# Weight conversion in a top-k attention + hard-swish kernel: one VectorE instruction per chunk instead of two, the sign word made on GpSimd

## The chip, the cores and the metric

One Trainium2 chip, one of its cores. The metric is the device time of one execution in microseconds (us). In profiles PE is TensorE, DVE is VectorE, ACT is ScalarE, POOL is GpSimd and SP is the engine whose queue issues most of the DMAs.

## What is computed

```python
def _attn_ref(q, k, v):                      # 8 batches, 8 heads, 576 rows, head size 64
    scores = scale * np.matmul(q, k.transpose(0, 1, 3, 2))
    kth = np.partition(scores, -top_k, axis=-1)[..., -top_k:-top_k + 1]      # top_k = 32
    scores = np.where(scores >= kth, scores, -1000000000.0)
    scores = scores - np.max(scores, axis=-1, keepdims=True)
    attn = np.exp(scores)
    attn = attn / (np.sum(attn, axis=-1, keepdims=True) + 1e-09)
    return np.matmul(attn, v).astype(np.float32)

def _moe_ref(x, w_in, w_out):                # x: 4608 x 512, the attention's output
    h = x @ w_in                             # 512 x 2048
    g = h * np.clip(h + 3.0, 0.0, 6.0) / 6.0
    return (g @ w_out).astype(np.float32)    # 2048 x 512
```

`w_in` and `w_out` arrive as 64-bit floats (a float32 matrix times a 64-bit scalar). The kernel reads them as pairs of 32-bit words and turns them into 32-bit floats itself. That conversion is what the change is about.

## The kernel before

**Attention.** The work is cut into 80 duos. A duo is 128 query rows (64 for the last, short row tile of a batch) of four heads, handled as two pairs, u = 0 and u = 1. Ten duos make a batch. For each duo TensorE forms the scores (L254 to L262), ScalarE copies them to SBUF (L271), and VectorE finds each row's 32 largest by four rounds of MAX8 (L283) with MATCH_REPLACE8 between them (L287). One round of one pair is a slot: a duo has 8 slots, numbered on over the kernel, so duo m has slots 8m to 8m+7. A slot's VectorE work is two MAX8 and two MATCH_REPLACE8, and in the fourth round of a pair (slots 3, 7, 11, 15 ...) the two MAX8 alone.

After a pair's fourth round: `shift` (two tiny GpSimd instructions, L296 and L299), `exp` (ScalarE, L306 to L316, which needs `shift` for its second half), `inverse` (a VectorE reciprocal, L320), `weights` (GpSimd: L330 scales the two rows, L339 splits their words into 16-bit halves), `flip` (a transposing DMA from SP's queue, L345), `join` (L351, on ScalarE or GpSimd), `values` (TensorE, L371) and `place` (ScalarE, L381). The slot of each is written out in the tables at L570 to L583. The first two duos use the table `early`: shift and exp in the fourth round's own slot, inverse and weights one slot later, flip one after that, join in slot 8 or 12.

**Feed-forward.** 36 blocks of 128 rows (L385). A block is four groups of 32 matmuls (L398), each with a ScalarE eviction (L406, L408) into a tile of the pool `g` and a gate of two GpSimd instructions (L412, L413), and then 16 matmuls with `w_out` (L418). Blocks are cut into pieces and about one piece is put into each slot.

**Conversion.** 32 chunks of 128x512 weights (16 of `w_in`, 16 of `w_out`). `convert` (L96) is a generator with three stops, and `convert_step` (L522), called once in each slot, moves it on. Chunk k has in the code before:

- its load (L103), a DMA into `st`, a tile of the pool `kq`, which also holds the attention's tiles;
- in slot k-2: ScalarE turns the low word into a rounding term `y` (L109; `y` is a PSUM tile for the first 24 chunks, the destination itself for the last 8), then takes the absolute value of the high word (L112) over the low word; GpSimd clamps that (L113);
- in slot k: VectorE shifts the clamped word left by 3 (L118), and a second VectorE instruction (L119) puts the high word's sign bit to `y` and writes the destination;
- in slot k+1: GpSimd adds the two as 32-bit integers (L124), which gives the float.

So the conversions run beside the first 33 slots. In slot s the order on each engine is: the top-k round; shift, exp, flip, join, values and place that are due; GpSimd's add for chunk s-1; VectorE's conversion of chunk s; ScalarE's and GpSimd's part for chunk s+2; the next load; then score matmuls or transposes; then inverse and weights. The order on every engine is the program's order (L68, `manual_schedule`); tiles of a pool take the buffer that has been free longest.

**Start.** `transpose(first=True)` (L189 to L202) turns the first pair's keys and queries on TensorE; ScalarE copies the results out (L195 to L197), and after `scores((0,))` (L267 to L271) it copies three blocks of scores, the small one (`rest`) first.

Of the kernel before, what the change touches and what calls it, by code (L numbers as in the profile page):

```python
# [8 lines left out]
AF = mybir.ActivationFunctionType  # L9
ALU = mybir.AluOpType  # L10
F32 = mybir.dt.float32
U32 = mybir.dt.uint32
I32 = mybir.dt.int32
# [11 lines left out]
HI_LEAST = 2.0**-15  # L25
HI_MOST = 122880.0 - 2.0**-7
# [3 lines left out]
def kernel(  # L30
# [9 lines left out]
    nc = tc.nc  # L40
    P = nc.NUM_PARTITIONS
# [3 lines left out]
    JP = J * P  # L45
    R = S - JP
    NHP = H // 2
    NFC = FF // P
    assert 2 * D == P and 2 * R == P and NHP * P == DM and B % 2 == 0
    assert JP == 512 and DM == 512 and TOP_K % 8 == 0  # L50
    scale = 1.0 / float(D) ** 0.5

    def pool(name, bufs, **kw):
        return ctx.enter_context(tc.tile_pool(name=name, bufs=bufs, **kw))
# [8 lines left out]
    gpool = pool("g", 8)  # L63
# [3 lines left out]
    ps_w = pool("ps_w", 3, space=PSUM)  # L67
# [20 lines left out]
    def big():  # L88

        return ps_big.tile([P, 5 * 512], F32, tag="big", name="big")  # L90
# [2 lines left out]

    WC = 512

    def convert(dst, src, early):  # L96

        st = kqpool.tile([P, 2 * WC], U32, tag="kq", name="st")
        nc.sync.dma_start(st[:], src)  # L103
        yield
        words = st[:].rearrange("p (n two) -> p n two", two=2)
        lo, hi = words[:, :, 0], words[:, :, 1]
        y = ps_w.tile([P, WC], F32, tag="w", name="y")[:] if early else dst

        nc.scalar.activation(y, lo, AF.Copy, bias=2.0, scale=2.0**-51)  # L109

        a = lo.bitcast(F32)
        nc.scalar.activation(a, hi.bitcast(F32), AF.Abs)  # L112
        nc.gpsimd.tensor_scalar(a, a, HI_MOST, HI_LEAST, ALU.min, ALU.max)  # L113
        yield

        nc.vector.tensor_scalar(lo, lo, 3, None, ALU.logical_shift_left)  # L118
        nc.vector.scalar_tensor_tensor(  # L119
            out=dst.bitcast(U32), in0=hi, scalar=0x80000000, in1=y.bitcast(U32),  # L120
            op0=ALU.bitwise_and, op1=ALU.bitwise_or,
        )
        yield
        nc.gpsimd.tensor_tensor(  # L124
            dst.bitcast(I32), lo.bitcast(I32), dst.bitcast(I32), ALU.add
        )

    def weight_chunks():
        win, wout = moe_w_in.bitcast(U32), moe_w_out.bitcast(U32)
        for f in range(0, FF, WC):  # L130
            for g in range(NHP):
                rows = slice(g * P, (g + 1) * P)
                yield w_in[:, g, f : f + WC], win[rows, 2 * f : 2 * (f + WC)]
        for c in range(NFC):
            rows = slice(c * P, (c + 1) * P)
            yield w_out[:, c, :], wout[rows, :]
# [3 lines left out]
    class Pair:  # L140
# [31 lines left out]

        def transpose(self, first=False):

            kq = kqpool.tile([P, JP + S], F32, tag="kq", name="kq")
            self.kT, self.qT = kq[:, 0:JP], kq[:, JP : JP + S]
            c0 = 2 * JP

            def turn(ps, tiles):
                for i, j in enumerate(tiles):  # L180
                    rows = self.landed[:, j, :, :].rearrange("p h d -> p (h d)")
                    nc.tensor.transpose(ps[:, i * P : (i + 1) * P], rows, ident[:])  # L182

            def copy_left(ps):
                for hh in range(2):
                    d = slice(hh * D, (hh + 1) * D)
                    nc.scalar.copy(self.kr[d, hh, :], ps[d, 0:R])

            if first:  # L189

                ps = [ps_w.tile([P, 512], F32, tag="w", name="kqp") for _ in range(3)]
                turn(ps[0], range(J))
                turn(ps[1], [J, 2 * J])
                turn(ps[2], range(J + 1, 2 * J))
                nc.scalar.copy(self.kT, ps[0][:])  # L195
                nc.scalar.copy(kq[:, JP : JP + P], ps[1][:, 0:P])
                copy_left(ps[1][:, P:])  # L197
                self.later = [
                    (kq[:, JP + P : c0], ps[2][:, 0 : JP - P]),
                    (kq[:, c0 : c0 + R], ps[1][:, P + R : 2 * P]),  # L200
                ]
                return  # L202
            ps = big()
            turn(ps, range(2 * J + 1))
            nc.scalar.copy(kq[:, 0:c0], ps[:, 0:c0])
            nc.scalar.copy(kq[:, c0 : c0 + R], ps[:, c0 + R : c0 + 2 * R])
            copy_left(ps[:, c0:])

    class Duo:
# [15 lines left out]
        def scores(self, us=(0, 1)):  # L225

            if us[0] == 0:
                self.sc = scpool.tile([P, 2, 2 * (S + R)], F32, tag="sc", name="sc")
                self.den = mpool.tile([P, 2, 2], F32, tag="den", name="den")
            sc, nu = self.sc[:, us[0] : us[-1] + 1, :], len(us)  # L230
            ps = big()
            heads = [slice(0, D), slice(D, P)]
            qs = slice(self.qt * P, min(self.qt * P + P, S))
            banks = ps[:, 0 : 4 * 512].rearrange("p (n s) -> p n s", s=512)
            left = ps[:, 4 * 512 :]
            if self.rest:


                quarters = [
                    (i, hh, d, heads[u ^ hh])  # L240
                    for i, u in enumerate(us)
                    for hh, d in enumerate(heads)
                ]
                for i, hh, d, to in quarters:
                    pr = self.pairs[us[i]]
                    nc.tensor.matmul(banks[to, i, :], pr.qT[d, qs], pr.kT[d, :])
                for i, hh, d, to in quarters:
                    pr = self.pairs[us[i]]
                    nc.tensor.matmul(banks[to, 2 + i, 0:R], pr.qT[d, qs], pr.kr[d, hh, :])
                nc.gpsimd.memset(sc[:, :, S : S + R], 0.0)  # L250
                nc.scalar.copy(sc[:, :, 0:JP], banks[:, 0:nu, :])
                nc.scalar.copy(sc[:, :, JP:S], banks[:, 2 : 2 + nu, 0:R])
                return
            for i, u in enumerate(us):  # L254
                pr = self.pairs[u]
                nc.tensor.matmul(  # L256
                    left[:, i * P : (i + 1) * P], pr.qT[:, qs], pr.kr[:].rearrange("p h r -> p (h r)")
                )
            for i, u in enumerate(us):
                pr = self.pairs[u]  # L260
                for hh, d in enumerate(heads):
                    nc.tensor.matmul(banks[:, 2 * i + hh, :], pr.qT[d, qs], pr.kT[d, :])  # L262
            copies = [
                (sc.rearrange("p u (h s) -> p (u h) s", h=2)[:, :, 0:JP], banks[:, 0 : 2 * nu, :]),
                (sc[:, :, JP : JP + P], left[:, 0 : nu * P].rearrange("p (u r) -> p u r", r=P)),
            ]
            if us == (0,):  # L267
                (to, src), rest = copies
                copies = [rest, (to[:, 0, :], src[:, 0, :]), (to[:, 1, :], src[:, 1, :])]
            for copy in copies:  # L270
                nc.scalar.copy(*copy)  # L271

        def row(self, u, t):
            return self.sc[:, u, t * S : (t + 1) * S]
# [237 lines left out]
    chunks = list(weight_chunks())  # L512
    landing, converting, adding = [], [], []

    def land(count=1):

        for _ in range(min(count, len(chunks))):
            c = convert(*chunks.pop(0), early=len(chunks) >= NFC // 2)
            next(c)
            landing.append(c)  # L520

    def convert_step():  # L522


        for c in adding:
            next(c, None)
        adding.clear()
        if len(converting) >= 2 or not landing:
            for c in converting[:1]:
                next(c)  # L530
            adding.extend(converting[:1])
            del converting[:1]
        if landing:
            c = landing.pop(0)
            next(c)
            converting.append(c)
        land()
# [10 lines left out]
    ps = big()  # L548
    for _ in range(2):
        nc.tensor.matmul(ps[:, 0:DM], w_out[:, 0, 0:P], w_out[:, 0, :])  # L550
    first[0].load(nc.scalar)
    first[1].load()
    land()
    first[2].load()
    land()
    first[0].transpose(first=True)
    duos[0].scores((0,))
    for copy in first[0].later:
# [17 lines left out]
    early = dict(  # L576
        shift0=3, exp0=3, inverse0=4, weights0=4, flip0=5, join0=8,
        shift1=7, exp1=7, inverse1=8, weights1=8, flip1=9, join1=12, values=12, place=13,
    )
# [98 lines left out]
```

## Time and profile before

| | |
|---|---|
| median of 7 runs | 1564.8 us (1563.7 to 1570.43) |
| profiled execution | 1564.29 us, span 1562.5 us |
| first chunk's GpSimd clamp, last chunk's add | 14.5 us, 147.6 us |
| VectorE's two conversion lines, L118 and L119 | 28.6 us + 23.4 us, 32 instructions each |
| ScalarE's two, L109 and L112 | 32 instructions each, medians 0.63 (PSUM) or 0.68 (SBUF), and 0.68 us |
| GpSimd's two, L113 and L124 | 32 instructions each, medians 0.65 and 1.30 us |
| GpSimd's idle time in front of L113, for L112 | 43.9 us, 15 times |
| last MAX8 ends | 1491.6 us; what follows is mostly feed-forward on TensorE |

A row of a timeline gives start, length, engine, line, operation, tiles and count; neighbouring instructions of one line are merged. The bracket is the time for which the engine was idle before, and what ended that. A VectorE or GpSimd instruction that is held up after it has started shows as a longer instruction, not as idle time.

### The profile page before, as it was taken

What the parts mean: (1) busy time and instruction counts of PE and PEld (TensorE: products, weight loads), DVE (VectorE), ACT (ScalarE), POOL (GpSimd) and SP (SyncE); (2) the same over time, 40 slices, a digit from 0 to 9 for tenths busy, and PEclk for the clock granted to TensorE, in tenths of its full rate; (3) what the DMA queues carried; (4) which work ended last, traced back from release to release, by engine and by line L of the source; (5) the groups of instructions that cost most, each with busy time, mean ns of one, the idle gap of its engine ahead of it and who ended that gap; (6) DMA issues with size and microseconds to landing.
All of it is one profiled execution on the core that took longest, in us unless ns stands there. A gap on an engine that the chain in (4) does not pass through costs nothing.

```text
span 1562.5 us, 28780 instructions
## 1 busy us (share of the span) xinstructions
PE 1444.9 (92%) x10276; PEld 1032.4 (66%) x10276; DVE 1464.5 (94%) x3106; ACT 1099.2 (70%) x1868; POOL 1138.0 (73%) x1264
## 2 busy tenths in 40 slices
PE   5256899899999999999999999999999999999899
PEld 3143665677777777667767777677777777666665
DVE  6999999999999998999999999999999999999910
ACT  6676777677777777777777776777777777777631
POOL 3769688677777788677777779777777778777761
PEclk7568799999999999999999999999999999999999
DMA  8553545344344445345344454554344545433320
GB/s 225 157 200 60 100 83 113 75 91 83 69 83 99 99 83 106 72 100 100 70 85 83 102 99 83 90 99 98 69 83 83 99 99 91 96 68 68 77 44 14
DMA packets 450319, 144.49 MB, mean 92 GB/s; under 512 B 433280, under 2 KB 441472, under 8 KB 450176
## 3 DMA queue, kind: packets, MB, share of 16 engines
q1 hardware_dynamic: 448976, 142.36, 44.3%
q8 instruction: 81, 1.33, 0.3%
q14 instruction: 62, 0.51, 0.1%
q10 hardware_dynamic: 1200, 0.30, 0.1%
HBM read 45.09 MB, written 9.44 MB: 35 GB/s over the span
## 4 chain that ended last, share of the span: by engine, by line
DVE 44%; PE 41%; POOL 5%; ACT 4%; issue 4%; DMA 1%; SPq 1%; POOLq 0%; DVEq 0%; ACTq 0%
DVE m L283 23%; DVE wk L287 19%; PE h L398 16%; PE acc L418 15%; PE pv L371 5%; PE big L262 3%; POOL e L339 1%; POOL sc L330 1%; ACT eT L351 1%; POOL eT L351 1%; PE big L182 1%; PE big L256 1%; ACT sc L311 1%; DMA t<-e 1%; DVE st L118 1%
## 5 line engine op out<-in xcount | busy, mean ns | idle before, releaser
L283 DVE MAX8 m<-wk 128x8 f32<-128x576 f32 x864 | 613.7, 748 | 2.2
L418 PE MATMUL acc<-w_out,g 128*128 128x512 f32 x1152 | 520.3, 602 | 11.9 <-POOL g L413 11.9
L398 PEld LDWEIGHTS h<-xT,w_in 128*128 128x128 f32 x4096 | 470.2, 193 | 39.6 <-issue 21.6
L398 PE MATMUL h<-xT,w_in 128*128 128x128 f32 x4096 | 483.2, 277 | 14.2 <-ACT xT L381 13.1
L287 DVE MATCH_REPLACE8 wk<-m,wk 128x576 f32<-128x576 f32 x576 | 424.0, 743 | 0.0
L418 PEld LDWEIGHTS acc<-w_out,g 128*128 128x128 f32 x1152 | 213.5, 192 | 256.7 <-issue 235.7
L330 POOL TENSOR_SCALAR sc<-sc,den 128x576 f32<-128x576 f32 x288 | 213.5, 751 | 202.6 <-DVE den L320 180.7
L339 POOL COPY e<-sc 128x2304 uint16<-128x2304 uint16 (+1 forms) x192 | 320.1, 1677 | 10.1
L351 ACT COPY eT<-t 128x2304 uint16<-128x2304 uint16 (+1 forms) x82 | 216.1, 2635 | 59.0 <-DMA t<-e 54.7
L306 ACT ACTIVATE sc<-sc,m 128x576 f32<-128x576 f32 x288 | 210.6, 779 | 66.2 <-DVE m L283 66.0
L311 ACT ACTIVATE sc<-sc,shift 128x576 f32<-128x576 f32 x288 | 220.5, 770 | 41.1 <-POOL shift L299 39.0
L371 PE MATMUL pv<-eT,vm 128*64 128x128 f32 (+1 forms) x2560 | 164.5, 273 | 58.2 <-DVE w_out L119 20.1
L283 DVE MAX8 m<-sc 128x8 f32<-128x576 f32 x288 | 203.4, 744 | 10.2 <-ACT sc L271 10.2
L287 DVE MATCH_REPLACE8 wk<-m,sc 128x576 f32<-128x576 f32 x288 | 212.0, 743 | 0.0
L351 POOL COPY eT<-t 128x2304 uint16<-128x2304 uint16 (+1 forms) x78 | 203.6, 2610 | 7.3 <-DMA t<-e 7.2
L371 PEld LDWEIGHTS pv<-eT,vm 128*64 128x64 f32 x2560 | 135.5, 141 | 109.9 <-issue 21.6
L406 ACT ACTIVATE g<-h,three 128x512 f32<-128x512 f32 x144 | 98.9, 687 | 135.7 <-PE h L398 135.4
L413 POOL TENSOR_TENSOR g<-g,hs 128x512 f32<-128x512 f32 x144 | 184.5, 1281 | 12.2 <-POOL g L412 0.2
L271 ACT COPY sc<-big 128x256 f32<-128x256 f32 (+3 forms) x131 | 136.5, 1095 | 26.4 <-PE big L262 26.1
L412 POOL TENSOR_SCALAR g<-g 128x512 f32<-128x512 f32 x144 | 88.7, 616 | 69.4 <-ACT g L406 59.6
L262 PE MATMUL big<-kq 64*128 64x512 f32 x512 | 133.0, 639 | 0.0
L408 ACT COPY hs<-h 128x512 f32<-128x512 f32 x144 | 83.8, 582 | 0.0
(58 smaller groups left out, 1001.7 us busy)
## 6 DMA issues: line engine op xcount, KB each, us to landing
landed<-in_k_dram SPq DMA_DIRECT2D x64, 128.0 KB, 2.9
st<-in_moe_w_in_dram SPq DMA_DIRECT2D x16, 512.0 KB, 5.3
vm<-in_v_dram SPq DMA_DIRECT2D x64, 128.0 KB, 2.4
st<-in_moe_w_out_dram SPq DMA_DIRECT2D x16, 512.0 KB, 5.2
out_dram<-o SPq DMA_DIRECT2D x32, 256.0 KB, 2.4
landed<-in_q_dram SPq DMA_DIRECT2D x62, 128.0 KB, 2.9
t<-e SPq DMA_TRANSPOSE x160, 4.6
landed<-in_k_dram SPq DMA_DIRECT2D x32, 32.0 KB, 2.5
```

The source lines that it names most:

```text
L262: nc.tensor.matmul(banks[:, 2 * i + hh, :], pr.qT[d, qs], pr.kT[d, :])
L283: nc.vector.max(self.m[u][:, t, 8 * r : 8 * r + 8], self.cur[t])
L287: nc.vector.match_replace(wk, self.m[u][:, t, 8 * r : 8 * r + 8], self.cur[t], LOWEST)
L306: nc.scalar.activation(row, row, AF.Prelu, bias=m[:, t, TOP_K - 1 : TOP_K], scale=-1.0, alpha=FLAT)
L311: nc.scalar.activation(row, row, AF.Exp, bias=self.less[u][:, t : t + 1], scale=-scale / FLAT, accum_out=self.den[:, u, t : t + 1],)
L330: nc.gpsimd.tensor_scalar(row, row, self.den[:, u, t : t + 1], 1.0, ALU.mult, ALU.mult)
L339: nc.gpsimd.tensor_copy(halves[:, :, to : to + c1 - c0], words)
L351: copy(eT[:, 0 : self.nb, :] .rearrange("p c q -> p (c q)") .bitcast(U16) .rearrange("p (x h) -> p h x", h=2), self.t16[u][:, 0 : 2 * self ...
L371: nc.tensor.matmul(pv[hh * D : (hh + 1) * D, u * w : (u + 1) * w], pr.vm[:, hh, c, :] if c < J else pr.vr[:, hh, :], rhs, start=(c == 0), ...
L398: nc.tensor.matmul(h[:, (f - f0) * P : (f - f0 + 1) * P], w_in[:, i, f * P : (f + 1) * P], xT[:, i, :], start=(i == 0), stop=(i == NHP - 1),)
L413: nc.gpsimd.tensor_tensor(g[:], g[:], hs[:], ALU.mult)
L418: nc.tensor.matmul(acc[:], gs[f // nf][:, f % nf * P : (f % nf + 1) * P], w_out[:, f, :], start=(f == 0), stop=(f == NFC - 1),)
```

## The change

Per chunk, the absolute value goes to a tile `a` of its own, from the feed-forward's pool `g` (8 buffers, tag `g`); the rounding term goes straight to the destination for all 32 chunks, so that no PSUM tile is used; and ScalarE does the absolute value first. GpSimd gets an instruction more: the high word, read as a float, times 0.0 leaves a zero with the high word's sign, written over the low word in `st`. VectorE's single instruction shifts `a` left by 3 and sets the sign with an exclusive-or. GpSimd's add stays as it was. At the start, two ScalarE lines and the first `rest` copy go to VectorE.

```diff
-    def convert(dst, src, early):
+    def convert(dst, src):
...
-        y = ps_w.tile([P, WC], F32, tag="w", name="y")[:] if early else dst
-
-        nc.scalar.activation(y, lo, AF.Copy, bias=2.0, scale=2.0**-51)
-
-        a = lo.bitcast(F32)
-        nc.scalar.activation(a, hi.bitcast(F32), AF.Abs)
-        nc.gpsimd.tensor_scalar(a, a, HI_MOST, HI_LEAST, ALU.min, ALU.max)
+        a = gpool.tile([P, WC], F32, tag="g", name="a")
+        nc.scalar.activation(a[:], hi.bitcast(F32), AF.Abs)
+        nc.gpsimd.tensor_scalar(a[:], a[:], HI_MOST, HI_LEAST, ALU.min, ALU.max)
+
+        nc.scalar.activation(dst, lo, AF.Copy, bias=2.0, scale=2.0**-51)
+
+        nc.gpsimd.tensor_scalar(lo.bitcast(F32), hi.bitcast(F32), 0.0, 1.0, ALU.mult, ALU.mult)
         yield
...
-        nc.vector.tensor_scalar(lo, lo, 3, None, ALU.logical_shift_left)
+        au = a[:].bitcast(U32)
         nc.vector.scalar_tensor_tensor(
-            out=dst.bitcast(U32), in0=hi, scalar=0x80000000, in1=y.bitcast(U32),
-            op0=ALU.bitwise_and, op1=ALU.bitwise_or,
+            out=au, in0=au, scalar=3, in1=lo,
+            op0=ALU.logical_shift_left, op1=ALU.bitwise_xor,
         )
         yield
         nc.gpsimd.tensor_tensor(
-            dst.bitcast(I32), lo.bitcast(I32), dst.bitcast(I32), ALU.add
+            dst.bitcast(I32), a[:].bitcast(I32), dst.bitcast(I32), ALU.add
         )
...
-            def copy_left(ps):
+            def copy_left(ps, copy=nc.scalar.copy):
                 for hh in range(2):
                     d = slice(hh * D, (hh + 1) * D)
-                    nc.scalar.copy(self.kr[d, hh, :], ps[d, 0:R])
+                    copy(self.kr[d, hh, :], ps[d, 0:R])
...
                 nc.scalar.copy(self.kT, ps[0][:])
-                nc.scalar.copy(kq[:, JP : JP + P], ps[1][:, 0:P])
-                copy_left(ps[1][:, P:])
+                nc.vector.tensor_copy(kq[:, JP : JP + P], ps[1][:, 0:P])
+                copy_left(ps[1][:, P:], nc.vector.tensor_copy)
...
             for copy in copies:
-                nc.scalar.copy(*copy)
+                if us == (0,) and copy is rest:
+                    nc.vector.tensor_copy(*copy)
+                else:
+                    nc.scalar.copy(*copy)
...
-            c = convert(*chunks.pop(0), early=len(chunks) >= NFC // 2)
+            c = convert(*chunks.pop(0))
```

## The prediction

> **What bounds the kernel now.** I read the page's busy table first, then the busy times by stretch, the conversion's own lines, and last the timeline of the conversion engine by engine.
>
> ```profile
> PE 1444.9 (92%) x10276; PEld 1032.4 (66%) x10276; DVE 1464.5 (94%) x3106; ACT 1099.2 (70%) x1868; POOL 1138.0 (73%) x1264
> ```
>
> Over the span VectorE is the fullest engine, with POOL far behind. But conversions run only from 14 to 148 us, and there the stretches (busy time of PE, PEld, DVE, ACT, POOL, then clock, DMA share, GB/s) say something else:
>
> ```profile
> 40.00:60.00 20.00, 1.58 (x6) 0.34 (x2) 20.00 (x34) 14.13 (x20) 15.67 (x18) 0.59 0.60 159
> ...
> 120.00:140.00 20.00, 15.74 (x46) 6.98 (x44) 19.16 (x34) 13.12 (x21) 19.25 (x19) 0.91 0.16 31
> 140.00:160.00 20.00, 11.46 (x59) 6.15 (x60) 20.00 (x44) 10.67 (x18) 18.82 (x19) 0.76 0.48 102
> 160.00:180.00 20.00, 12.84 (x88) 10.83 (x85) 20.00 (x44) 14.30 (x26) 11.01 (x13) 0.65 0.45 90
> ```
>
> VectorE is "full" at 20.00 of 20, but POOL has 15.67, and 19.25 near the end. VectorE's fullness isn't all work:
>
> ```profile
> L118 DVE TENSOR_SCALAR st<-st x32: 404/620/1976, 15.2 to 139.4; 128x512 uint32<-128x512 uint32 x32
> ...
> L119 DVE SCALAR_TENSOR_TENSOR w_in<-st,y x16: 673/675/682, 15.5 to 76.3; 128x512 uint32<-128x512 uint32 x16
> ...
> L119 DVE SCALAR_TENSOR_TENSOR w_out<-st,w_out x8: 678/886/1151, 110.6 to 139.8; 128x512 uint32<-128x512 uint32 x8
> ```
>
> The shift needs 404 ns and takes up to 1976: it is held while POOL works (the one at 54.89 ends at 56.83, when POOL's copy L339 has ended at 56.54). So VectorE has slack that shows as busy time. Who sets the pace is seen in four slots of POOL's timeline:
>
> ```profile
> 60.73 0.19 POOL L296 TENSOR_TENSOR shift<-m 128x2 f32<-128x2 f32 x1
> 61.01 0.22 POOL L299 TENSOR_SCALAR shift<-shift 128x2 f32<-128x2 f32 x1
> 61.20 1.30 POOL L124 TENSOR_TENSOR w_in<-st,w_in 128x512 int32<-128x512 int32 x1
> 64.45 0.65 POOL L113 TENSOR_SCALAR st<-st 128x512 f32<-128x512 f32 x1 [1.96 <-ACT st L112]
> 65.06 1.29 POOL L124 TENSOR_TENSOR w_in<-st,w_in 128x512 int32<-128x512 int32 x1
> 68.32 0.65 POOL L113 TENSOR_SCALAR st<-st 128x512 f32<-128x512 f32 x1 [1.97 <-ACT st L112]
> 69.07 1.47 POOL L330 TENSOR_SCALAR sc<-sc,den 128x576 f32<-128x576 f32 x2
> 70.60 2.10 POOL L339 COPY e<-sc 128x2304 uint16<-128x2304 uint16 x1
> 72.67 1.47 POOL L124 TENSOR_TENSOR w_in<-st,w_in 128x512 int32<-128x512 int32 x1
> 74.22 0.65 POOL L113 TENSOR_SCALAR st<-st 128x512 f32<-128x512 f32 x1
> 74.83 1.29 POOL L124 TENSOR_TENSOR w_in<-st,w_in 128x512 int32<-128x512 int32 x1
> 76.09 0.83 POOL L113 TENSOR_SCALAR st<-st 128x512 f32<-128x512 f32 x1
> 76.88 0.20 POOL L296 TENSOR_TENSOR shift<-m 128x2 f32<-128x2 f32 x1
> ```
>
> From shift to shift it is 16.15 us, and POOL is idle twice, both times for ScalarE. In both waits ScalarE has no gap: after the shift (61.20) come two exponentials, the sum's copy, L109, L112 (to 64.37), the join of 2.75, L109, L112 (to 68.24). The MAX8 that the next shift needs ended at 58.74, 2.0 us ahead of 60.73. So from slot 7 to slot 19 the pace is a loop of POOL and ScalarE; VectorE isn't in it.
>
> **The change part by part.**
>
> *VectorE.* Removed: L118, 28.6 us, and L119, 23.4 us. Added: 32 instructions with both inputs in SBUF. Their nearest row is L119 on `w_out`, 678 to 1151 ns, mean 904 (page of groups by shape): 32 x 0.904 = 28.9. Saved: 52.0 - 28.9 = 23.1 us. Worth that only where VectorE sets the pace, so I take 0 from slot 7 on. The Trainium skill, "VectorE: DVE Perf Modes", section "Rules for kernel authors", says to minimise the number of chained VectorE instructions. The row agrees about VectorE's own time, but the loop above leaves VectorE out; by the rule alone the time would be that of the first rival below.
>
> *POOL, the product.* 32 more instructions. Nearest rows: the clamp L113 on the same words, 0.65 us, and the gate's L412 on dense words, 0.616; so 0.65, 20.8 us in all. What of it is covered, by its place in the four slots: in the first slot (after shift) it waits for ScalarE's L109, but the second 1.97 wait covers it. In the second slot the product follows the clamp, and the clamp comes 0.65 earlier, since the absolute value now runs before the rounding term; cost 0. In the third and fourth slot POOL has no idle time: 2 x 0.65 = 1.30. Back comes what L118 made slower: the add of 1.47 for 1.29 and the clamp of 0.83 for 0.65, 0.35. So +0.95 in each cycle, if nothing collides.
>
> *Collisions.* Where L119 with two SBUF inputs runs beside POOL, POOL is slower: an add takes 1.74 for 1.30 (119.61, 137.59), the two scalings 2.04 and 2.27 for 1.47 (122.06, 139.42). Four VectorE conversions fall in a cycle. Two meet POOL in front of its waits, and are covered. The one in the first slot waits for the third slot's product and so starts beside the next add, +0.44; another falls on L339 or L330, +0.57. From below the cost is 0, so a cycle gains 0.95 to 1.95; with most of them colliding I take 1.5. The Trainium skill, "GPSIMD Engine Reference", section "8. Key points", names just this: SBUF interfaces are shared with VectorE's instructions that have two SBUF inputs. By the rule every one of them collides and the cycle is +1.95; if it did not hold, +0.95.
>
> *ScalarE.* 24 rounding terms go to SBUF: 0.68 for 0.63, and in the loop only once per cycle; 0.05, left out. The PSUM buffer that they free ends no wait of this loop. `a` takes the buffer of `g` free longest; with at most seven of eight in use it waits for an add two chunks back, which POOL has done by then.
>
> *Loads.* `st` is free after VectorE instead of after the add; the loads' order on SP's queue is the same, and no more of them. 0.
>
> *Start.* One 128x128, two 64x64 and one 128x128 copy move to VectorE, idle for 10.21 us there. No row shows VectorE copying from PSUM; between the reciprocal's 0.155 and the 128x512 memset's 0.485 each, so 0.6 to 1.9 in all; ScalarE is rid of 0.27 + 0.43 + about 0.3. The first MAX8 (11.62) may come between 0.9 earlier and, at the dear end, 0.9 later. Neither lasts: the reciprocal at 32.70 waits 1.71 for ScalarE's L316, and ScalarE waits before that for loads (13.07, 17.16). I take 0.
>
> **The sum.** Slots 5 to 7: three products without cover, 3 x 0.65 = 1.95 on POOL; VectorE loses nothing yet. Slots 7 to 15, two cycles: 2 x 1.5 = 3.0. The weights of slot 16 are 4.95 late. From there the path is L339 (ends 88.82), the flip, the join (94.77), values, xT (101.73), the first h matmul (102.23): all 4.95 late. In slots 20 to 24 POOL waits 5.18, 1.79 and 1.70 us for ScalarE, which waits for the join and for h; the products hide there, and the lag stays 4.95. From 114.74 to 152.9 POOL has no idle time. Five more products (chunks 27 to 31) are 3.25, more collisions than the rows there already have 0 to 2.2, I take 0.7: 8.9. The last product ends at 137.59 + 8.9 = 146.5, VectorE's last conversion takes 0.6 to 1.05, and the next MAX8 starts at 147.3 instead of 140.36: 6.9 late. With 0.95 per cycle and no collisions (2.3 us of those in the present rows gone too) it is 2.6 late, with all of them 9.5.
>
> After that, POOL's rest of lag (8.9 against VectorE's 6.9) goes into its 5.12 us of idle time at 160.4. TensorE's pieces at 165.45 and 172.90 wait 4.22 and 2.93 for ScalarE and POOL, which wait for MAX8; so from 173 on everything stands as before, 6.9 later, and stays so, since TensorE and VectorE both run without slack. The profiled execution took 1564.29 (1.8 outside its span, 0.5 under the median): 1564.3 + 6.9 = 1571.2, so 1571; own range 1567 to 1574.
>
> **The rivals.**
>
> 1. *VectorE is the bound after all.* Then 23.1 us come off: 1541.2; half of it where only part of the slots pay, 1553. For it: 20.00 of 20 busy from 40 to 120 us, and slots 20 to 24, where L118 is mostly near 0.41 and POOL waits. Against: the 2.0 us between MAX8 and shift, and L118's 1.98 for 0.40. It decides if POOL's cycle falls under 16.15. 15%.
> 2. *The products are covered.* POOL waits 43.9 us for L112, twice the 20.8; then only chunks 27 to 31 are paid or not: 1564.3 - 2.4 (six unblocked shifts at 0.41 in slots 17 to 23) to + 3.2: 1562 to 1567.5. Against: the waits lie in two of four slots, and none from 114.74 on. 20%.
> 3. *Collisions without cover.* If each of 24 conversions from slot 8 to 31 delays POOL by 0.44 to 0.80, mean 0.6, that is 14.4, with the uncovered products (1.95 + 2.6 + 3.25 = 7.8) 22 on POOL, some 18 on VectorE: 1582. For it: POOL is nearly always busy. Against: L113 and L330 at present lose less on average. 10%.
>
> **How the numbers follow.** The forecast has 55%. A run can tell 0.2%, 3.1 us, from no change. Slower than that: 10% and all but 5 of the 55; within: those 5 and rival 2; faster: rival 1. The range leaves out about half of rival 1 below and rival 3 above: 1556 to 1578.
>
> **What would show it.** Right: POOL's shift-to-shift cycle near 17.6 between slots 7 and 19; VectorE idle in front of the new conversion, for POOL's product, about 3 us per cycle (it now shows as idle, not as a long shift); the conversion's mean near 0.9; POOL above 18 of 20 us from 40 to 140; the last add starting near 156.5; the MAX8 after the last conversion near 147. Wrong: the cycle at 16.2 or less, VectorE without idle time, or a product far from 0.65. If conversion ends as computed and the total still differs, the step from 173 us on is wrong.

## The result, and the profile after

The changed kernel takes 1570.17 us (median; 1569.12 to 1571.53) against 1565.23 us for the kernel before in the same comparison: ratio 1.0027, 95% interval 1.0019 to 1.0035, so 0.3% or some 4 to 5 us slower. The profiled execution took 1568.75 us (span 1567.0) against 1564.29 (span 1562.5), +4.5 us.

The busy table of the kernel after:

```profile
PE 1443.6 (92%) x10276; PEld 1031.3 (66%) x10276; DVE 1450.9 (93%) x3078; ACT 1095.7 (70%) x1864; POOL 1159.5 (74%) x1296
```

VectorE lost 13.6 us of busy time, GpSimd gained 21.5 us, and the kernel is slower by less than either. The stretches of the kernel after (busy time of PE, PEld, DVE, ACT, POOL, each with its number of instructions, then clock, DMA share, GB/s):

```profile
40.00:60.00 20.00, 3.13 (x22) 2.00 (x20) 13.62 (x25) 12.97 (x19) 16.78 (x20) 0.50 0.50 140
...
100.00:120.00 20.00, 17.41 (x121) 15.47 (x122) 20.00 (x40) 16.88 (x33) 18.01 (x23) 0.75 0.61 244
120.00:140.00 20.00, 14.60 (x65) 8.96 (x66) 15.61 (x26) 12.89 (x23) 18.94 (x21) 0.83 0.16 30
140.00:160.00 20.00, 12.76 (x44) 5.28 (x40) 18.75 (x36) 9.35 (x15) 19.27 (x21) 0.74 0.30 63
160.00:180.00 20.00, 9.10 (x73) 6.94 (x75) 20.00 (x45) 13.88 (x26) 12.32 (x12) 0.78 0.63 130
```

VectorE is no longer full in most of the conversion's stretch: 13.62 of 20 where it had 20.00. From 100 to 120 us it still is. GpSimd went from 15.67 to 16.78 only, so it still waits, too. What VectorE waits for is in the rows of the new conversion (its instructions, then its engine's idle time in front of them):

```profile
L118 DVE SCALAR_TENSOR_TENSOR a<-a,st x32: 674/894/1768, 13.8 to 144.6; 128x512 uint32<-128x512 uint32 x32
...
  POOL st L112: 22.4, 8
```

22.4 us in eight waits, all for GpSimd's product (L112). GpSimd's timeline over four slots of the kernel after, from one `shift` to that four slots later:

```profile
63.94 0.20 POOL L301 TENSOR_TENSOR shift<-m 128x2 f32<-128x2 f32 x1
64.22 0.22 POOL L304 TENSOR_SCALAR shift<-shift 128x2 f32<-128x2 f32 x1
64.40 1.27 POOL L123 TENSOR_TENSOR w_in<-a,w_in 128x512 int32<-128x512 int32 x1
66.97 0.61 POOL L108 TENSOR_SCALAR a<-a 128x512 f32<-128x512 f32 x1 [1.30 <-ACT a L107]
67.66 0.66 POOL L112 TENSOR_SCALAR st<-st 128x512 f32<-128x512 f32 x1
68.27 1.28 POOL L123 TENSOR_TENSOR w_in<-a,w_in 128x512 int32<-128x512 int32 x1
70.72 0.61 POOL L108 TENSOR_SCALAR a<-a 128x512 f32<-128x512 f32 x1 [1.16 <-ACT a L107]
71.41 0.66 POOL L112 TENSOR_SCALAR st<-st 128x512 f32<-128x512 f32 x1
72.04 1.98 POOL L335 TENSOR_SCALAR sc<-sc,den 128x576 f32<-128x576 f32 x2
74.09 2.10 POOL L344 COPY e<-sc 128x2304 uint16<-128x2304 uint16 x1
76.15 1.26 POOL L123 TENSOR_TENSOR w_in<-a,w_in 128x512 int32<-128x512 int32 x1
77.51 0.61 POOL L108 TENSOR_SCALAR a<-a 128x512 f32<-128x512 f32 x1
78.20 0.64 POOL L112 TENSOR_SCALAR st<-st 128x512 f32<-128x512 f32 x1
78.80 1.26 POOL L123 TENSOR_TENSOR w_in<-a,w_in 128x512 int32<-128x512 int32 x1
80.15 0.94 POOL L108 TENSOR_SCALAR a<-a 128x512 f32<-128x512 f32 x1
81.16 0.65 POOL L112 TENSOR_SCALAR st<-st 128x512 f32<-128x512 f32 x1
81.77 0.20 POOL L301 TENSOR_TENSOR shift<-m 128x2 f32<-128x2 f32 x1
```

From shift to shift it is 17.83 us; it was 16.15. There is a product in each slot. The one at 67.66 lies in front of a wait for ScalarE (1.16 of the former 1.97 are left), and the one at 71.41 stands where the later clamp used to end. Those at 78.20 and 81.16 have no wait in front of them or behind them, and the next shift is later by both. VectorE's conversions in the same slots:

```profile
72.81 0.68 DVE L118 SCALAR_TENSOR_TENSOR a<-a,st 128x512 uint32<-128x512 uint32 x1
73.42 1.41 DVE L288 MAX8 m<-wk 128x8 f32<-128x576 f32 x2
78.88 1.74 DVE L118 SCALAR_TENSOR_TENSOR a<-a,st 128x512 uint32<-128x512 uint32 x1 [4.05 <-POOL st L112]
```

VectorE is idle for 4.05 us until the product of 78.20 has ended, and its conversion then takes 1.74 us, because GpSimd's add started at 78.80. The conversion ends only after that add has ended (80.06).

### The profile page after: what moved, and what is told of

Its sections match the earlier page's. It is cut to its first block, busy times and chain, and to the rows that moved or that the text cites. A ratio compares the mean times of both kernels' runs of the same rounds, so it can differ in the third digit from the quotient of the medians.

```text
span 1567.0 us, 28761 instructions
## 1 busy us (share of the span) xinstructions
PE 1443.6 (92%) x10276; PEld 1031.3 (66%) x10276; DVE 1450.9 (93%) x3078; ACT 1095.7 (70%) x1864; POOL 1159.5 (74%) x1296
## 4 chain that ended last, share of the span: by engine, by line
PE 55%; DVE 22%; POOL 11%; ACT 5%; issue 5%; DMA 2%; POOLq 0%; SPq 0%; ACTq 0%
PE h L403 22%; PE acc L423 20%; DVE m L288 12%; DVE wk L292 10%; PE pv L376 6%; PE big L264 5%; POOL e L344 2%; POOL sc L335 2%; DMA t<-e 1%; POOL eT L356 1%; PE big L258 1%; POOL g L418 1%; PE big L184 1%; POOL w_in L123 1%; ACT sc L316 1%
## 5 line engine op out<-in xcount | busy, mean ns | idle before, releaser
L403 PE MATMUL h<-xT,w_in 128*128 128x128 f32 x4096 | 484.8, 278 | 12.7 <-ACT xT L386 11.9
L276 ACT COPY sc<-big 128x2048 f32<-128x2048 f32 (+3 forms) x130 | 136.4, 1101 | 25.9 <-PE big L264 23.1
```

The costliest lines, as they stand in the source:

```text
L403: nc.tensor.matmul(h[:, (f - f0) * P : (f - f0 + 1) * P], w_in[:, i, f * P : (f + 1) * P], xT[:, i, :], start=(i == 0), stop=(i == NHP - 1),)
```

## The experiments

The table gives, for every kernel, what it did to the time and where it gained or lost: the start of VectorE's reciprocals (one for each pair of rows; the first four are in slots 4, 8, 12 and 16, the seventh is near the last conversion, and from there on all kernels have the same 9.70 us from one to the next). The cycle is the distance of the third and the fourth. The change in us is the ratio's distance from 1, times 1565.2. The ratio comes from all runs of a kernel, the columns behind it from one execution; executions of one kernel lie 1 to 9 us apart, so small differences in the columns say little.

| kernel | ratio to before (95%) | us | cycle | 2nd | 4th | 5th | 6th | 7th |
|---|---|---|---|---|---|---|---|---|
| before | 1 | 0 | 16.2 | 48.35 | 80.63 | 114.90 | 133.67 | 145.91 |
| after | 1.0027 (1.0019 to 1.0035) | +4.2 | 17.8 | 48.46 | 84.20 | 118.47 | 138.17 | 151.85 |
| no product (e1) | 0.9949 (0.9937 to 0.9961) | -8.0 | 15.9 | 46.72 | 78.44 | 110.76 | 128.10 | 140.23 |
| product in the kernel before (e2) | 1.0089 (1.0077 to 1.0101) | +13.9 | 18.3 | 49.94 | 86.45 | 125.15 | 146.81 | 161.02 |
| start copies only (e3) | 0.9996 (0.9988 to 1.0005) | -0.6 | 16.2 | 47.82 | 80.12 | 114.46 | 133.62 | 145.85 |
| own tile only (e9) | 1.0003 (0.9994 to 1.0012) | +0.5 | 15.8 | 47.92 | 79.45 | 114.16 | 131.80 | 144.47 |
| own tile and order (e7) | 0.9977 (0.9968 to 0.9985) | -3.6 | 15.3 | 46.72 | 77.33 | 113.35 | 132.35 | 146.66 |
| e7 and start (e8) | 0.9985 (0.9974 to 0.9996) | -2.3 | 15.3 | 47.15 | 77.76 | 113.74 | 132.71 | 147.00 |
| after with the old order (e18) | 1.0053 (1.0040 to 1.0066) | +8.3 | 18.4 | 49.65 | 86.54 | 122.02 | 141.68 | 155.39 |
| PSUM operand (e4) | 1.0029 (1.0018 to 1.0040) | +4.5 | 17.0 | 48.34 | 82.40 | 117.88 | 139.38 | 153.09 |
| PSUM operand, `st` free (e4b) | 1.0013 (1.0004 to 1.0022) | +2.0 | 17.0 | 48.82 | 82.83 | 115.68 | 137.22 | 150.92 |
| product on VectorE (e5) | 1.0025 (1.0015 to 1.0035) | +3.9 | 16.5 | 48.31 | 81.30 | 118.59 | 136.04 | 150.53 |
| late products (e14) | 1.0083 (1.0070 to 1.0096) | +13.0 | 16.4 | 53.10 | 85.90 | 121.19 | 141.66 | 159.38 |
| e8, PSUM for all chunks (e17) | 0.9947 (0.9935 to 0.9959) | -8.3 | 15.3 | 47.62 | 78.22 | 112.12 | 127.77 | 139.61 |

**What does the product cost?** e1 is the changed kernel without it; the conversion reads a block of zeros in SBUF in its place, so it still has two SBUF inputs.

```diff
-        nc.gpsimd.tensor_scalar(lo.bitcast(F32), hi.bitcast(F32), 0.0, 1.0, ALU.mult, ALU.mult)
...
-            out=au, in0=au, scalar=3, in1=lo,
+            out=au, in0=au, scalar=3, in1=zeros,     # shortened: a block of w_out that holds zeros
```

> The changed kernel without GpSimd's product; VectorE's instruction takes a block of zeros in SBUF as its second input, so all weights lose their sign. Theory (a loop of GpSimd and ScalarE sets the pace, the product lengthens it): the cycle from shift to shift between slots 7 and 19 falls from 17.9 us to 16.2 to 16.6, and the time from 1570.2 to 1561 to 1565. Rival (VectorE's instruction with two SBUF inputs is what costs, not the product): the cycle stays near 17.5 and the time at 1568 to 1570.

Measured: 1557.97 us, 12.2 us under the kernel after by the ratios, more than expected, and the cycle falls from 17.8 to 15.86, below the expected 16.2 to 16.6. The groups of the run without product:

```profile
L118 DVE SCALAR_TENSOR_TENSOR a<-a,w_out 128x512 uint32<-128x512 uint32 x32 | 33.9, 1061 | 9.9 <-POOL a L109 9.8
```

The conversion's mean, 1061 ns, stays what it was (1076 after), so it isn't quicker conversions that give the gain: of some 21 us of GpSimd's time for the product (32 of them, median 0.656) 12.2 reach the end. In e1 `st` also comes free sooner, as VectorE no longer reads it; in the kernel after the join of slot 20 waited for its own data alone (row below), so no gain from that is seen. VectorE's wait falls from 22.4 to 9.9 us.

e2 is the kernel before with the product as additional work, after the clamp; the conversion on VectorE stays as it was.

```diff
         nc.gpsimd.tensor_scalar(a, a, HI_MOST, HI_LEAST, ALU.min, ALU.max)
+        nc.gpsimd.tensor_scalar(hi.bitcast(F32), hi.bitcast(F32), 0.0, 1.0, ALU.mult, ALU.mult)
```

> The kernel before, with the product added on GpSimd behind the clamp (high word times 0.0 in place; the sign that the second VectorE instruction takes stays the same). Theory: three products per cycle are uncovered here, as the absolute value still comes second on ScalarE: cycle 16.15 + 1.95 = 18.1 us, time 1565.2 + 6 to 9 = 1571 to 1574. Rival (the product hides in GpSimd's waits and the harm came from the new VectorE instruction): 1565 to 1567.

Measured: +13.9 us. The cycle, 18.26, is as expected; the total isn't. The lateness grows behind the cycles, from 5.8 at the fourth reciprocal to 10.3 at the fifth and 15.1 at the seventh, where the expectation let it stand. In this kernel `st` is held until the add, and the join of slot 20 comes 7.4 us behind the copy that it follows; before it was 5.95, after 4.69. So the product alone, with nothing of the rest of the change, slows the kernel by more than the whole change does, and the rest of the change has to be a gain.

**Which part gains?** Start copies alone (e3), the own tile `a` alone (e9), own tile and absolute value first (e7), both with the start (e8), each put into the kernel before, and the old order put into the kernel after (e18).

```diff
 e9, in the kernel before
-        a = lo.bitcast(F32)
+        a = gpool.tile([P, WC], F32, tag="g", name="a")[:]
 e7, in addition
-        nc.scalar.activation(y, lo, AF.Copy, bias=2.0, scale=2.0**-51)
         nc.scalar.activation(a, hi.bitcast(F32), AF.Abs)
         nc.gpsimd.tensor_scalar(a, a, HI_MOST, HI_LEAST, ALU.min, ALU.max)
+        nc.scalar.activation(y, lo, AF.Copy, bias=2.0, scale=2.0**-51)
 e18, in the kernel after
+        nc.scalar.activation(dst, lo, AF.Copy, bias=2.0, scale=2.0**-51)
         nc.scalar.activation(a[:], hi.bitcast(F32), AF.Abs)
...
-        nc.scalar.activation(dst, lo, AF.Copy, bias=2.0, scale=2.0**-51)
```

> The kernel before, with only the three start copies on VectorE. Theory: the first MAX8 comes 1 us earlier and the reciprocal of slot 4 about 1.3 earlier, as in the changed kernel, and here nothing eats it: 1565.2 - 1.3 = 1564. Rival (loads pace the start, as the prediction had it): 1565, with the reciprocal at 32.7 us.

> The kernel before, with only the absolute value in a tile of pool g; ScalarE's order as before. Cycle 16.15 us as before; the join in slot 20 1.2 us earlier; time 1563 to 1565. If st's early release is all that made the kernel without the product fast: 1558 to 1560. If neither counts: 1565.8.

> The kernel before, with both its VectorE instructions and no product, but the absolute value in a tile of pool g and first on ScalarE. Theory: both waits of GpSimd for the absolute value end 0.65 us earlier, one of them counts: cycle 15.5 to 15.9 us; the join in slot 20 comes 1.2 us earlier because VectorE, not GpSimd's add, frees st; time 1558 to 1561, as with VectorE's one instruction and no product. Rival (VectorE's saving counts): 1563 to 1565.

> The kernel before with the absolute value in a tile of pool g and first on ScalarE, and the three start copies on VectorE: the parts of the change without the product and without VectorE's one instruction. Theory: the start adds nothing to the 1560.8 us of the order alone, so 1560 to 1561. Rival: the start's 0.6 to 1.3 us at slot 4 lasts once GpSimd's loop is shorter: 1559 to 1560.

> The changed kernel with ScalarE's two instructions in the old order, rounding term first. Theory (ScalarE is in the loop): the absolute value comes 0.65 us later, the second slot's product is no longer covered: cycle 18.5 us, time 1572 to 1575. Rival (with GpSimd this full the order no longer counts): 1570.

Measured: start copies -0.6 us with an interval that holds 0: the first MAX8 comes at 10.58 for 11.62, and nothing of it is left by the seventh reciprocal (-0.06). The own tile +0.5, no change, although the join of slot 20 comes 2.7 us earlier with it (92.03 for 94.77). With the order as well -3.6, and the old order in the kernel after costs 4.1 us: the order is worth about 4 us in both kernels. e8 adds nothing to e7 that its interval would show; at 1562.9 it is slower than its expectation. Runs of e7 scatter from 1559.2 to 1564.67 us and the profiled one is the longest; no run here shows why. Eight of its eleven runs end at 1561.0 or before, five of e8's twelve at 1560.6 or before, and the profiled one of e8 took 1564.93: the rows of both show a late execution.

What is left is VectorE's one instruction. e1 has it, with the order and the start, and no product; e8 has the order and the start and two instructions. e1 is 5.6 us faster (0.9949 and 0.9985, intervals apart). By the profiled executions (that of e8 a late one) this comes behind slot 19: at its shift e8 is still 2.2 us ahead of e1 (89.27 for 91.45), at the seventh reciprocal 6.8 behind. So VectorE's shorter work, taken at 0 by the prediction from slot 7 on, seems to count there; that e1 also frees `st` sooner and takes no PSUM tile isn't separated from it. With the product in, e18 is 5.6 us ahead of e2, both with the old order: own tile, start and the one instruction together, which no run separates there.

e7's cycle is 15.3, but its lead of 3.3 us at the fourth reciprocal turns into 0.75 of lateness at the seventh. Its conversions that have no PSUM operand, the last eight, say where to look (first row; the second has 16 of those with a PSUM operand):

```profile
L118 DVE SCALAR_TENSOR_TENSOR w_out<-st,w_out 128x512 uint32<-128x512 uint32 x8 | 13.3, 1666 | 0.0
L118 DVE SCALAR_TENSOR_TENSOR w_in<-st,y 128x512 uint32<-128x512 uint32 x16 | 10.8, 675 | 0.0
```

1666 ns in the mean with two SBUF inputs (904 in the kernel before), 675 with one input in PSUM. e17, below, follows that up.

**What do the collisions cost?** e4 lets the conversion of the first 24 chunks read its second operand from PSUM, as the kernel before did; the product is still made, and the add's second input is the product. The sign is left out.

```diff
+        y = ps_w.tile([P, WC], F32, tag="w", name="y")[:] if early else lo.bitcast(F32)
-        nc.scalar.activation(dst, lo, AF.Copy, bias=2.0, scale=2.0**-51)
+        nc.scalar.activation(y if early else dst, lo, AF.Copy, bias=2.0, scale=2.0**-51)
...
-            out=au, in0=au, scalar=3, in1=lo,
+            out=au, in0=au, scalar=3, in1=y.bitcast(U32),
...
-            dst.bitcast(I32), a[:].bitcast(I32), dst.bitcast(I32), ALU.add
+            dst.bitcast(I32), a[:].bitcast(I32), (lo if early else dst).bitcast(I32), ALU.add
```

> The changed kernel, with the second input of VectorE's instruction in PSUM for the first 24 chunks (the rounding term, as before the change; the sign word goes to GpSimd's add instead, and these weights come out with the other sign and unrounded). All instruction counts as in the changed kernel. If two SBUF inputs are what collides: the conversion takes 0.67 us in place of up to 1.75, the clamps of 0.94 and scalings of 2.0 go back to 0.61 and 1.47, the cycle from 17.9 to 17.0 us, the time to 1566 to 1568. If the product alone is the cause: cycle 17.6 or more and 1569 to 1570. If the collisions are all of it: 16.2 and 1562 to 1565.

Measured: the cycle is 17.02 as the collision theory has it, but the time is that of the kernel after. ScalarE's join in slot 20, first in the PSUM kernel, then in the kernel after:

```profile
98.81 2.78 ACT L357 COPY eT<-t 128x2304 uint16<-128x2304 uint16 x1 [6.27 <-POOL w_out L124]
```

```profile
98.78 2.78 ACT L356 COPY eT<-t 128x2304 uint16<-128x2304 uint16 x1 [4.36 <-DMA t<-e]
```

1.8 us earlier at the fourth reciprocal, and no earlier at the join. In e4 the add reads `st`, so that the buffer which the join's tile `eT` takes comes free only after GpSimd's add (L124). In the kernel after VectorE is its last reader, and the join waits for nothing but its own data. e4 had put in one thing more than it took out. e4b lets the add read a block of zeros instead:

```diff
-            dst.bitcast(I32), a[:].bitcast(I32), (lo if early else dst).bitcast(I32), ALU.add
+            dst.bitcast(I32), a[:].bitcast(I32), (zeros if early else dst).bitcast(I32), ALU.add
```

> The changed kernel, VectorE's second input in PSUM for the first 24 chunks, GpSimd's add with a block of zeros for these (their weights come out unrounded and with the wrong sign), so that st is not held until the add. Collisions between VectorE and GpSimd gone in slots 7 to 19: cycle 17.0 us instead of 17.9, the join in slot 20 near 96 us instead of 98.8, time 1567 to 1568.5. If collisions don't count for the end: 1570.

Measured: 1567.55 us, within the expected interval; the join is at 96.79. Collisions in the first 24 chunks cost 0.85 us of each cycle: in the kernel after the clamp of 0.94 loses 0.33 (80.15) and the pair of scalings of 1.98 loses 0.51 (72.04), and in e4b they take 0.61 and 1.47. In the time it is 2.2 us (1.0027 - 1.0013), with intervals that just touch.

**Would the product be free elsewhere?** e5 makes it on VectorE, which waits for 22 us in the kernel after. e14 moves 12 of the 32 products (chunks from 8 on with k % 4 = 3 or 0, those without cover) two slots later, in front of the conversion, where GpSimd waits for ScalarE.

```diff
 e5
-        nc.gpsimd.tensor_scalar(lo.bitcast(F32), hi.bitcast(F32), 0.0, 1.0, ALU.mult, ALU.mult)
...
+        nc.vector.tensor_scalar(lo.bitcast(F32), hi.bitcast(F32), 0.0, 1.0, ALU.mult, ALU.mult)
         au = a[:].bitcast(U32)
 e14
+        late = k >= 8 and k % 4 in (3, 0)
+        if not late:
+            nc.gpsimd.tensor_scalar(lo.bitcast(F32), hi.bitcast(F32), 0.0, 1.0, ALU.mult, ALU.mult)
         yield
+        if late:
+            nc.gpsimd.tensor_scalar(lo.bitcast(F32), hi.bitcast(F32), 0.0, 1.0, ALU.mult, ALU.mult)
         au = a[:].bitcast(U32)
```

> The changed kernel with the product on VectorE, in front of its conversion instruction; so VectorE has two instructions again (0.40 and 1.08 us) and GpSimd as many as before the change. Theory (only GpSimd's and ScalarE's loop counts): GpSimd's cycle as without the product, 15.9 us, time 1558 to 1561. Rival (without the product it was VectorE's shorter work that gave 1558): VectorE's saving is gone, 1564 or more.

> The changed kernel with the same 32 products, but from chunk 8 on those of the third and fourth slot of each cycle are issued two slots later, behind the next add, where GpSimd waits 1.30 and 1.18 us for the absolute value. Theory (a product costs where nothing covers it): cycle from 17.9 to 16.6 us between slots 7 and 19; from slot 24 on there are no such waits, and VectorE gets its sign words later there; time 1565 to 1568. Rival (GpSimd's amount of work counts, not the place): cycle 17.9 and 1570.

Both theories missed, and e5 lies where its rival had it (1564 or more). e5 takes 1569.35 us, 11.9 us more than e1 by the ratios, so the product costs on VectorE what it costs on GpSimd. Its cycle is short (16.5), and its loss comes later: 0.7 us behind the kernel before at the fourth reciprocal, 3.7 at the fifth, 4.6 at the seventh. VectorE's conversion rows of this kernel and two of its stretches:

```profile
L118 DVE SCALAR_TENSOR_TENSOR a<-a,st 128x512 uint32<-128x512 uint32 x32 | 33.2, 1039 | 3.3
...
L116 DVE TENSOR_SCALAR st<-st 128x512 f32<-128x512 f32 x32 | 20.0, 625 | 0.0
```

```profile
80.00:100.00 20.00, 5.83 (x44) 4.91 (x44) 19.48 (x36) 16.07 (x22) 15.31 (x15) 0.51 0.67 210
100.00:120.00 20.00, 18.93 (x142) 16.30 (x143) 19.48 (x37) 17.10 (x32) 14.83 (x16) 1.00 0.34 135
```

VectorE is full again, 19.48 of 20. The wait of 22.4 us was the product's own shadow; with the product on VectorE it is gone, and there is nothing to fill. So a shorter loop of GpSimd and ScalarE isn't enough: the loss comes behind it, with VectorE full. That VectorE's work is the reason is argued from these rows.

e14 reached the cycle that cover would give, 16.4, but VectorE's conversion now needs a product that GpSimd makes just in front of it (the releaser's rows under VectorE's conversion, then one of them):

```profile
  POOL st L120: 32.0, 12
  POOL st L114: 5.8, 4
```

```profile
81.40 0.69 DVE L122 SCALAR_TENSOR_TENSOR a<-a,st 128x512 uint32<-128x512 uint32 x1 [3.30 <-POOL st L120]
```

32.0 us of waits for twelve late products. Against the kernel before, VectorE is set back once by 4.75 us (second reciprocal, 53.10), and by another 8 between the fourth and the seventh. GpSimd's waits cover the product's own time, and VectorE pays for its lateness.

**A version that beats both.** e17 leaves the product away and keeps both VectorE instructions: e8 with the rounding term in PSUM for all 32 chunks, so that no conversion has two SBUF inputs. It computes everything.

```diff
-            c = convert(*chunks.pop(0), early=len(chunks) >= NFC // 2)
+            c = convert(*chunks.pop(0), early=True)
```

> As the kernel with the absolute value first and the start copies, with the rounding term in PSUM for all 32 chunks instead of 24, so that the second VectorE instruction of the last 8 takes 0.68 us and not 1.67. If their collisions are what takes back the 3.3 us that kernel is ahead in slot 17: 1557 to 1559. If the three PSUM tiles are then short for the feed-forward, which starts in slot 21: 1562 or more.

Measured: 1556.79 us, 8.3 us faster than before and 12.5 faster than after by the ratios. The lead at the fourth reciprocal isn't lost any more but grows to 6.3 at the seventh. Its last sixteen chunks:

```profile
L118 DVE SCALAR_TENSOR_TENSOR w_out<-st,y 128x512 uint32<-128x512 uint32 x16 | 10.8, 674 | 0.0
```

674 for 1666 ns. And it is as fast as e1 (0.9947 and 0.9949), which has one VectorE instruction where e17 has two: what e1 gains over e8 behind slot 19 can be had without the one instruction, and isn't a matter of the count. It is 5.9 us faster than e8 by the ratios; that the collisions are the reason is read from one execution of each.

## Why the prediction was right

The forecast was slower by 6.9 us, through a loop of GpSimd and ScalarE that the product lengthens while VectorE's saving is worth nothing there. Measured were 4.2 us by the ratios and 4.5 by the profiled executions. The direction stands, and so does the mechanism for slots 7 to 19: e1 and e2 put the price of the product at 12.2 and 13.9 us, and the cycle is 17.0 to 18.4 us wherever GpSimd makes the products in their place and 15.3 to 16.2 where there are none. For the slots behind 19 it is only partly right, and that the size came out so near is in part luck, since terms that were too small and too large offset each other. Point by point:

- **"From slot 7 to slot 19 the pace is a loop of POOL and ScalarE; VectorE isn't in it."** Shown for these slots: VectorE lost 4 to 6 us of 20 of busy time from 40 to 100 us and the cycle became longer. In e17, with one instruction more on VectorE than e1, the cycle isn't longer either (15.3 and 15.9). The Trainium skill, "VectorE: DVE Perf Modes", section "Rules for kernel authors", has the count of chained VectorE instructions minimised; here two instructions (e17) are as fast as one (e1), and what an instruction is held up by brought the time. Past slot 19 the step is too wide: in e5, e7 and e14 the losses come there with VectorE full or waiting, and e8 against e1 points the same way.
- **The cycle, +1.5.** Measured 17.83 to 17.91, +1.7. Cover in two slots and none in the other two is as predicted; e18 shows that the second slot's cover comes from the order on ScalarE (18.4 without it). The collisions' part, 0.55 taken of 0 to 1.0, is 0.85 by e4b, and the rest 0.87 for 0.95. The adds, which the prediction had slower by 0.44, aren't: VectorE waits for them, and the clamp and the scalings lose the time.
- **Slots 5 to 7, +1.95.** Measured +1.44 at the shift of slot 7 (46.03 for 44.59), but from a lead of 1.3 at the first reciprocal (31.38 for 32.70), so these slots took more than the 1.95. The start was taken at 0; of that lead the start copies alone give 0.5 (e3, 32.16), and e7, without them, has 0.7 (32.04). At the shift of slot 15 it was +4.89, for 4.95: a lead left out, slots and cycles put too low, and a sum that fits by luck.
- **"Loads. `st` is free after VectorE instead of after the add ... 0."** This is a term that was mis-sized. It isn't the loads that gain by it but the join: its tile takes that buffer, and in the kernel before the join of slot 20 waited for GpSimd's add, not for the flip:

```profile
94.77 2.78 ACT L351 COPY eT<-t 128x2304 uint16<-128x2304 uint16 x1 [3.65 <-POOL w_out L124]
```

In the kernel after it is 4.0 late instead of 4.95 (98.78 for 94.77). e4 and e4b show the size the other way round, 2 us at the join and 2.5 in the time (1.0029 - 1.0013); in e9 the earlier join alone shortens nothing.
- **Slots 20 to 33.** Predicted: last product ends at 146.5, next MAX8 at 147.3, +6.9. Measured: 144.6 and 146.30, +5.94. The product is 1.9 less late than predicted, of which the join's 0.95 may be a half (argued, not tried); VectorE's one instruction, taken at 0 here, is another candidate; the last conversion gave some of it back, with 1.74 where 0.6 to 1.05 were assumed.
- **VectorE's saving, 23.1 us.** 52.0 us of lines became 34.4, so 17.6: the mean is 1076 ns, not 904. In slots 7 to 19 it made no difference, as VectorE had time there. For the slots behind, the prediction gave no row for its 0, and without the product e1 is 5.6 us faster than e8; what it is worth with the product in, no run shows alone.
- **"6.9 later, and stays so."** Wrong by a quarter. The 5.94 last until 598 us, where 1.47 of them go: VectorE's reciprocal waits there for ScalarE, which was late by less. The rows of this wait, kernel before, then after, from 540 to 620 us:

```profile
L320 DVE RECIPROCAL den<-den 128x1 f32<-128x1 f32 x5 | 0.8, 155 | 5.0 <-ACT den L316 5.0
```

```profile
L325 DVE RECIPROCAL den<-den 128x1 f32<-128x1 f32 x5 | 0.8, 156 | 3.5 <-ACT den L321 3.5
```

A wait of VectorE, 5.0 us before and 3.5 after, took up the difference; the last reciprocal is 4.46 late (1501.96 for 1497.50), and so is the end. "Without slack" overlooks this wait; one of 5 us in 1500 can't be seen in a busy share.
- **What would show it.** Cycle, idle VectorE (4.1 us per cycle, 3 said) and MAX8 near 147 came; "POOL above 18 of 20 from 40 to 140" didn't (16.6 to 16.8 up to 100 us), since two waits per cycle stayed. The last add started some 3 us before the 156.5 said (153.6).

Still open: why e7 and e8 scatter more than the others, what share of e17's gain over e8 falls to which of the last sixteen chunks, and what VectorE's one instruction is worth behind slot 19 with the product in.

## What to carry to other kernels

An engine that shows as full may be held up by another one; before work is taken off it, find the loop that sets the pace (here, shift to shift on GpSimd up to slot 19) and ask where in it the new work has a wait to hide in. Do so for each stretch anew: behind slot 19 the kernels that lost time had VectorE full or waiting (e5, e7, e14). Work that is moved has a price at its place and one by its lateness: the product cost 12 us on GpSimd, as much on VectorE, and more when 12 of the 32 were put into GpSimd's waits. Cheap gains lay beside it: the instruction that another engine waits for goes first, and an operand in PSUM instead of SBUF keeps two engines apart.

## What the runs showed of the hardware

- Of a VectorE conversion with two SBUF inputs and a GpSimd instruction beside it, the one that comes second waits for the other to end, and the first isn't slowed. In the kernel after it is mostly VectorE behind an add: 1.74 us for 0.67, beside an add of 1.26 (rows at 78.88 and 78.80 above). A GpSimd instruction with one input holds it up in the same way: the conversion of the second row below takes 1.04 and ends 0.54 after the clamp of the first. In e7 one takes 2.59 (119.26), behind a GpSimd copy of 16-bit halves that runs from 119.09 to 121.30.

```profile
107.94 0.61 POOL L108 TENSOR_SCALAR a<-a 128x512 f32<-128x512 f32 x1
108.05 1.04 DVE L118 SCALAR_TENSOR_TENSOR a<-a,st 128x512 uint32<-128x512 uint32 x1
```

- Where the conversion comes first, GpSimd pays: an add that started at 141.47, behind a conversion that started at 141.01, took 1.71; a clamp that the end of a conversion falls on takes 0.94 for 0.61 (80.15); the conversion at 72.81, just as the first of two scalings ends, takes 0.68, and the pair (72.04) takes 1.98 instead of 1.47. The prediction knew this kind alone, at 0.44 for an add. The Trainium skill, "GPSIMD Engine Reference", section "8. Key points", says that GpSimd shares its SBUF interfaces with VectorE and contends with its instructions that have two SBUF inputs; the runs agree, and show besides that the later one waits.
- With one of the two inputs in PSUM, the conversion takes 674 to 680 ns in the mean (e4b, e17), 672 to 689 one by one, beside GpSimd instructions or not.
